# V gathered in rows of 2 KB, weights in rows of 4 KB, another plan for the transfers, and unused products in TensorE's pauses

## The chip, the cores and the metric

One core of one Trainium2 chip. The metric is the device time of one execution in microseconds (us), as a median over runs. The core has five engines that run their own instruction streams: TensorE (PE, whose weight loads the profile lists apart as PEld), VectorE (DVE), ScalarE (ACT), GpSimd (POOL) and SyncE (SP). They wait for each other by semaphores. Transfers are issued by SP, ACT or POOL and carried out by 16 DMA engines that all three share.

## What is computed

Block-sparse attention with 4 batches, 8 heads, 768 positions in 24 blocks of 32, and 64 elements per head, then an MLP from 512 to 2048 to 512:

```python
mask = np.abs(blk_i - blk_j) <= 1
mask = mask | (blk_i == 0) | (blk_j == 0) | (blk_i == n_blocks - 1) | (blk_j == n_blocks - 1)
for qb in range(n_blocks):
    for kb in sampled_blocks[qb]:            # three per block, known at run time only
        mask[qb * 32:(qb + 1) * 32, kb * 32:(kb + 1) * 32] = True
scores = np.where(mask, scale * q @ k.T, -1e9)
attn = softmax(scores)
x = (attn @ v).transpose(0, 2, 1, 3).reshape(B * S, H * D)
h = x @ w_in
out = (h / (1 + exp(-beta * h))) @ w_out
```

Each block of queries between the first and the last looks at 8 blocks of keys: the first, the last, three around it, and three drawn ones. The first and the last block of queries look at all keys.

## The kernel before

**Attention, pair by pair.** Two neighbouring blocks of queries make a pair; a batch has 11 pairs (44 in all). A pair n goes through these steps, which are also the names of the planner's tasks:

- `kg` (line 515, POOL) and `kn` (524, POOL or DVE) copy the drawn and the fixed blocks of K out of `KT` into `KG`.
- `vv` (549, SP) loads the drawn block numbers into registers, and `vg` (579, SP) gathers V's rows by DMA from a table `VT` in DRAM into `VG`: 7 transfers for most pairs, 9 for the first of a batch. `VG` is 128 partitions x 2 (the blocks of the pair) x 2 (halves of the keys) x 512, so one row of V, 1 KB, lies in one partition. The first and the last block are gathered once a batch, and `vres` (589) copies them into the other `VG` buffers.
- `sc` (595, PE) makes the scores, with a product of `ones` and `maskr` (line 600) that masks repeated blocks; `mx` (621, DVE) the maxima, `ex` (629, ACT) the exponentials, `rc` (635) and `nrm` (641, POOL or DVE) the scaling.
- `tp` (647, PE) transposes the probabilities, `ptv` (657, DVE) copies them out of PSUM, `av` (661, PE) multiplies with `VG`, and `xv` (678) writes the result to `xT`.

The first and last block of each batch go through `gs`, `gm`, `ge`, `gn`, `gt`, `gptv` and `gav` in the same manner (lines 694 to 777), with V from `Vn`.

**Getting a batch in.** Batch 0's Q, K and V are loaded as fp32 by SP at the start (line 388) and cast. Batches 1 to 3 are loaded by POOL with a cast into two staging buffers `RAW` (443), in the order V, K, Q; K shares a buffer with nothing, V and Q share the other. `perm` tasks on DVE put the rows in order (447), `trK` and `trQ` on PE transpose (460), `evK` and `evQ` copy to `KT` and `QT`. V in order (`Vn`) is written to the table `VT` by SP (`vtab`, 490 for batch 0 in two halves of the columns, 494 for the others).

**The MLP** runs over 8 groups of 256 or 512 tokens. `h` (814, PE, products at 817) makes one 128-row slice of the hidden layer out of `xT`, `tanh` (822, ACT) and `stt` (827, DVE) the activation, `y` (842, PE, products at 845) the output, `oe` (854) scales it out of PSUM, `od` (861) stores it. `w_in` and `w_out` come by POOL's DMA with a cast, in 16 pieces of 64 partitions, each row 8 KB of fp32 (417, 423). `h` waits for all eight pieces of `w_in`.

**The order** of all instructions is made on the host by a planner (`Plan`, line 36). Each task has an engine (or a choice of two), a duration, a priority and what it depends on; the planner runs a list schedule over modelled engines and 8 PSUM banks, and the kernel then issues the instructions in the planned order, engine by engine. The MLP may hold at most `moe_banks` banks (4) while attention is going on. In the planner's model all transfers pass through one ring, one after the other (`ring_at`); those of SP and ACT also take turns on 8 lanes, and POOL's large loads (`bulk`) are held back while the ring is more than `THR` us behind. The durations steer the order only; on the chip each instruction starts when its semaphores let it.

Of the kernel before, what the change touches and what calls it, by code (L numbers as in the profile page):

```python
# [22 lines left out]
class Task:  # L23
    def __init__(self, name, eng, dur, emit, deps=(), prio=0.0, lat=0.0,
                 opens=(), closes=(), moe=False, dma=0.0, slack=0.0, hw=0, bulk=None):
        self.on = {eng: dur} if isinstance(eng, str) else dict(eng)
        self.name, self.eng, self.dur, self.emit = name, None, None, emit
        self.deps = [d for d in deps if d is not None]
        self.prio, self.lat = prio, lat
        self.opens, self.closes, self.moe, self.dma = opens, closes, moe, dma  # L30
        self.slack, self.hw, self.bulk = slack, hw, bulk
        self.kind = name.rstrip("0123456789.")
        self.end = None


class Plan:
# [4 lines left out]
    def __init__(self, n_banks, moe_banks):  # L41
        self.tasks = []
        self.n_banks, self.moe_banks = n_banks, moe_banks
        self.bank = {}

# [5 lines left out]
    def run(self):  # L51
# [16 lines left out]
        ring_at = 1.0  # L68
        lanes = [0.0] * 8
# [18 lines left out]
        while done < len(tasks):  # L88
            progress = False
            for e in engines:  # L90
# [3 lines left out]
                for t in waiting[e]:  # L94
# [7 lines left out]
                    if t.bulk is not None and ring_at > now + t.bulk + 1e-9:  # L102
                        continue
# [14 lines left out]
                if t.opens:  # L118
                    bank_free.sort()
                    for name in t.opens:  # L120
                        _, i = bank_free.pop(0)
                        self.bank[name] = i
                        if t.moe:
# [6 lines left out]
                if t.hw:  # L130
                    at = now
                    for _ in range(t.hw):
                        at = max(at, lanes[issued % 8]) + t.dur / t.hw
                        ring_at = max(ring_at, at + 0.4) + t.dma / t.hw
                        end = lanes[issued % 8] = ring_at + 0.9
                        issued += 1
                    free[e] = at
                elif t.dma:
                    ring_at = max(ring_at, end + 0.6) + t.dma
                    end = ring_at + 1.1  # L140
                t.start, t.end = now, end
                order.append(t)
                heapq.heappush(events, (end, seq, t))
                seq += 1
# [8 lines left out]
            for e in engines:  # L153
                nxt += [ready_at[t] for t in waiting[e] if ready_at[t] > now + 1e-9]
                nxt += [ring_at - t.bulk for t in waiting[e]
                        if t.bulk is not None and ring_at - t.bulk > now + 1e-9]
            nxt += [f for f, _ in bank_free if f > now + 1e-9]
            if not nxt:
                raise RuntimeError("plan is stuck: " + ", ".join(
                    t.name for e in engines for t in waiting[e]))  # L160
            now = max(now, min(nxt))
            while events and events[0][0] <= now + 1e-9:
# [3 lines left out]
                done += 1  # L166
                for s in succ.get(t, ()):
# [5 lines left out]
                for b in t.closes:  # L173
                    readers[b] -= 1
                    if readers[b] == 0:
                        bank_free.append((t.end + self.HOP, self.bank[b]))
                        if b in moe_owner:
                            held_moe -= 1
        return order


@with_exitstack
def kernel(
# [52 lines left out]
    VG = [sb(f"VG{i}", [P, 2, 2, D_MODEL]) for i in range(NVG)]  # L236
# [13 lines left out]
    plan = Plan(8, 4)  # L250
# [39 lines left out]
    t_sbl = add("sbl", "ACT", 0.5, emit_sbl, prio=-200, dma=0.3, hw=1)  # L290
# [46 lines left out]
    for part, f in enumerate((emit_mask0, emit_mask1, emit_mask2)):  # L337
# [9 lines left out]
    beta_row = osb[0][0:4, :]  # L347
    ident32 = t_sb[1][0:4, 0:8].bitcast(FP32)
    FQ = N_FFC // 4
    t_beta0 = add("beta", "ACT", 0.5, lambda: nc.scalar.dma_start(  # L350
        out=beta_row, in_=moe_beta.rearrange("(q x) -> q x", q=FQ)), prio=-140, dma=0.1, hw=1)
    t_id32 = add("id32", "DVE", 0.2, lambda: nc.vector.tensor_copy(
        out=ident32, in_=identity[0:4, 0:4]), deps=[t_ident], prio=-64)

    def emit_betaT():
        for i in range(4):
            nc.tensor.transpose(out=bank("beta")[:, i * FQ:(i + 1) * FQ],
                                in_=beta_row.rearrange("q (p i) -> q i p", i=4)[:, i, :], identity=ident32)
# [3 lines left out]
        out=beta_sb[:, :].rearrange("x (q i) -> x i q", i=4),  # L362
        in0=bank("beta")[:, 0:N_FFC].rearrange("x (i q) -> x i q", i=4),
# [22 lines left out]
    for i, (nm, t, dst) in enumerate((("K", k, K16), ("Q", q, Q16), ("V", v, None))):  # L386
        for f in range(2):
            tl = add(f"ld{nm}0.{f}", "SP", 0.47, lambda i=i, t=t, f=f: nc.sync.dma_start(
                out=stage_half(i, f) if i < 2 else v_stage[:, f * HH:(f + 1) * HH, :],
                in_=src6(t, 0, f * HH, HH)), prio=-80 + i * 2 + f, dma=2.0, hw=1)  # L390
# [17 lines left out]

    w_in_r = moe_w_in.rearrange("(c p) f -> c p f", p=P)
    w_out_r = moe_w_out.rearrange("(q p i) m -> q p (i m)", p=P, i=4)  # L410
    w_in_v = w_in_sb[:, :, :].rearrange("x c (q p i) -> x c q i p", p=P, i=4)
    t_win, t_wout = [], []
    THR = 3.2
    for c in range(4):
        for f in range(2):
            ps = slice(64 * f, 64 * f + 64)
            t_win.append(add(f"win{c}.{f}", "POOL", 0.85, lambda c=c, ps=ps: nc.gpsimd.dma_start(
                out=w_in_sb[ps, c, :], in_=w_in_r[c, ps, :]),
                deps=[tch], prio=-50 + 0.2 * c + 0.1 * f, dma=1.3, bulk=THR))
    for c in range(4):  # L420
        for f in range(2):
            ps = slice(64 * f, 64 * f + 64)
            t_wout.append(add(f"wout{c}.{f}", "POOL", 0.85, lambda c=c, ps=ps: nc.gpsimd.dma_start(
                out=w_out_sb[ps, 4 * c:4 * c + 4, :].rearrange("x i m -> x (i m)"), in_=w_out_r[c, ps, :]),
                deps=[tch], prio=-49 + 0.2 * c + 0.1 * f, dma=1.3, bulk=THR))
# [7 lines left out]
    for b in range(B):  # L433
        pr = prep_prio(b)
        if b:
            vperm[b] = []
            for nm, t, raw, dst in (("V", v, RAW[0], Vn[b % 2]), ("K", k, RAW[1], K16), ("Q", q, RAW[0], Q16)):
                tr = {"K": trK, "Q": trQ}.get(nm)
                for f in range(2):
                    hs = slice(f * HH, (f + 1) * HH)  # L440
                    free = [vperm[b][f]] if nm == "Q" else [perm["QK"["VK".index(nm)], b - 1, f]] if b > 1 else []
                    tl = add(f"ld{nm}{b}.{f}", "POOL", 0.9, lambda t=t, raw=raw, b=b, f=f, hs=hs:
                             nc.gpsimd.dma_start(out=raw[:, hs, :], in_=src6(t, b, f * HH, HH)),
                             deps=free + [t_wout[-1]] if b == 1 else free,
                             prio=(-40 if b == 1 else pr - 30) + "VKQ".index(nm) + 0.5 * f, dma=2.55, bulk=THR)
# [36 lines left out]
        if b == 0:  # L482
            vperm[0], vtab[0] = [], []
            for f in range(2):
# [5 lines left out]
                vtab[0].append(add(f"vtab0.{f}", "SP", 0.45, lambda cs=cs, vt_rows=vt_rows: nc.sync.dma_start(  # L490
                    out=vt_rows[:, :, cs], in_=Vn[0][:, :, cs]),
                    deps=[vperm[0][f]], prio=-64, dma=1.3, hw=1))
        else:
            vtab[b] = [add(f"vtab{b}", "SP", 0.4, lambda b=b, vt_rows=vt_rows: nc.sync.dma_start(
                out=vt_rows, in_=Vn[b % 2]), deps=vperm[b], prio=pr + 5, dma=1.9, slack=1.0, hw=1)]
# [7 lines left out]
    for n, (b, p) in enumerate(order_pairs):  # L503
# [53 lines left out]

        def moves(vgb=vgb, vt=vt, i0=i0, first=head_v):
            if first:
                for s, blk in ((0, 0), (1, NB - 1)):  # L560
                    yield 0.25, lambda v, s=s, blk=blk: (
                        vgb[s * BLK:(s + 1) * BLK, :, 0, :],
                        bass.AP(tensor=vt.tensor, offset=vt.offset + blk * BLK * D_MODEL,
                                ap=[[D_MODEL, BLK], [0, 2], [1, D_MODEL]]))
            if i0 + 1 < NB - 2:
                yield 0.6, lambda v: (
                    vgb[BLK:P, :, 1, :],
                    bass.AP(tensor=vt.tensor, offset=vt.offset + (i0 - 1) * BLK * D_MODEL,
                            ap=[[D_MODEL, 3 * BLK], [BLK * D_MODEL, 2], [1, D_MODEL]]))
            else:  # L570
                yield 0.3, lambda v: (vgb[BLK:P, 0, 1, :], vt[(i0 - 1) * BLK:(i0 + 2) * BLK, :])
                yield 0.1, lambda v: (vgb[BLK:2 * BLK, 1, 1, :], vt[(NB - 1) * BLK:NB * BLK, :])
                yield 0.2, lambda v: (vgb[2 * BLK:P, 1, 1, :], vt[i0 * BLK:(i0 + 2) * BLK, :])
            for g in range(2):
                for r, (c, s) in enumerate(((0, 2), (0, 3), (1, 0))):
                    yield 0.1, lambda v, g=g, r=r, c=c, s=s: (
                        vgb[s * BLK:(s + 1) * BLK, g, c, :], vt[bass.ds(v[3 * g + r], BLK), :])
# [326 lines left out]
```

## Time and profile before

| | |
|---|---|
| median of 3 runs | 324.45 us (322.56 to 332.4) |
| the profiled execution | 323.59 us, span from the first to the last instruction 321.8 us |
| busy, share of the span | PE 280.7 us (87%), DVE 246.7 (77%), ACT 216.8 (67%), POOL 187.5 (58%) |
| mean granted clock of PE | 0.929 of full speed |
| chain that ended last | PE 60%, DMA 14%, DVE 12%, ACT 6% |

The profile names a group of instructions by line, engine, operation and tiles, so `PE bank L817` is the MLP's first product and `DMA VG<-VT` a gather of V. Idle time before an instruction is put down to what ended it. PE's clock is granted by a throttle, and the same product takes up to twice as long at half clock. The costliest groups on PE are the MLP's products, 97.1 us (512 products, line 817) and 90.9 us (384, line 845). DVE's are the maxima (57.5 us, line 621) and the activation (66.6 us, line 828).

### The profile page before, as it was taken

Reading aid. Unit: us, or ns where it says so; the run is one execution under the profiler, and the core shown is the slowest. Engines: PE = TensorE matmul, PEld = TensorE weight load, DVE = VectorE, ACT = ScalarE, POOL = GpSimd, SP = SyncE. Lnnn points to the kernel's source line nnn. Section 1 sums busy time; section 2 is a strip of 40 time slices with the busy share of each in tenths; the row PEclk is TensorE's granted clock in tenths of the full one; section 3 lists DMA queues with packets and bytes.
Section 4 is the critical chain, followed back from the end, with each engine's and each line's share of the span. In section 5 each row is a group of like instructions: output and inputs, shape, how many; then the busy total and the mean of one; then the engine's idle time right before and its main releaser. Section 6 shows DMA issues by size and latency. Waiting matters only on the chain.

```text
span 321.8 us, 10665 instructions
## 1 busy us (share of the span) xinstructions
PE 280.7 (87%) x3525; PEld 177.3 (55%) x3525; DVE 246.7 (77%) x572; ACT 216.8 (67%) x644; POOL 187.5 (58%) x528
## 2 busy tenths in 40 slices
PE   0845578989979699988979999999999999999994
PEld 0612366956755486556635656555665555554671
DVE  2996579878869989999987667999979975771060
ACT  1676435864968489789687669977679864772361
POOL 2479956848778456798966654756948453200000
PEclk9975557999979989999979999999999999999999
DMA  7889995998697586323777973335232333100201
GB/s 255 332 172 208 229 227 105 187 252 177 132 204 145 164 212 114 107 80 94 125 146 168 226 170 93 88 84 153 94 118 69 91 110 100 33 3 33 98 2 66
DMA packets 42211, 43.97 MB, mean 137 GB/s; under 512 B 6440, under 2 KB 37672, under 8 KB 42156
## 3 DMA queue, kind: packets, MB, share of 16 engines
q1 hardware_dynamic: 27760, 25.71, 27.1%
q0 software_dynamic: 10784, 11.27, 23.4%
q10 hardware_dynamic: 3612, 6.30, 5.4%
q8 instruction: 28, 0.46, 0.6%
q14 instruction: 27, 0.22, 0.2%
HBM read 45.10 MB, written 9.44 MB: 169 GB/s over the span
## 4 chain that ended last, share of the span: by engine, by line
PE 60%; DMA 14%; DVE 12%; ACT 6%; issue 3%; SPq 3%; POOL 1%; POOLq 0%; ACTq 0%; DVEq 0%
PE bank L845 22%; PE bank L817 21%; DMA VG<-VT 6%; PE bank L668 4%; PE bank L653 4%; DMA RAW<-in_k_dram 3%; DMA VT<-Vn 3%; SPq L582 3%; DVE ST L621 2%; ACT PP L629 2%; PE bank L463 2%; DVE g L828 2%; PE bank L610 2%; PE bank L600 2%; DMA sbl<-in_sampled_blocks_dram 1%
## 5 line engine op out<-in xcount | busy, mean ns | idle before, releaser
L641 POOL TENSOR_SCALAR PP<-PP,ST 128x256 f16<-128x256 f16 x168 | 81.3, 501 | 47.9 <-DVE ST L635 42.4
L629 ACT ACTIVATE PP<-bank,ST 128x256 f16<-128x256 f32 x176 | 81.6, 478 | 30.1 <-DVE ST L621 21.5
L817 PE MATMUL bank<-xT,w_in_sb 128*128 128x256 f16 (+1 forms) x512 | 97.1, 338 | 3.9 <-ACT PP L629 1.1
L845 PE MATMUL bank<-w_out_sb,g 128*128 128x512 f16 x384 | 90.9, 380 | 0.0
L828 DVE SCALAR_TENSOR_TENSOR g<-t,bank 128x512 f16<-128x512 f16 (+1 forms) x128 | 66.6, 546 | 22.1 <-ACT t L823 21.3
L823 ACT ACTIVATE t<-bank,beta_sb 128x512 f16<-128x512 f32 (+1 forms) x128 | 69.9, 589 | 14.3 <-PE bank L817 11.6
L817 PEld LDWEIGHTS <-w_in_sb 128*128 128x128 f16 x512 | 55.3, 116 | 30.1 <-issue 8.6
L521 POOL COPY KG<-KT 128x64 f32 x264 | 54.6, 256 | 24.6 <-PE bank L610 17.8
L621 DVE TENSOR_REDUCE ST<-bank 128x2 f32<-128x512 f32 x88 | 57.5, 678 | 7.5 <-PE bank L610 7.4
L845 PEld LDWEIGHTS <-g 128*128 128x128 f16 x384 | 34.7, 98 | 38.6 <-issue 4.1
L668 PE MATMUL bank<-PT,VG 128*128 128x64 f16 x704 | 31.8, 199 | 7.9 <-DMA VG<-VT 5.9
L668 PEld LDWEIGHTS <-VG 128*128 128x128 f16 x704 | 28.3, 102 | 16.5 <-issue 9.6
L629 ACT ACTIVATION_READ_ACCUMULATOR PP<-bank,ST 128x1 f32 x176 | 36.8, 209 | 0.0
L653 PE MATMUL bank<-identity,PP 128*128 128x128 f16 x352 | 30.9, 233 | 6.6 <-ACT xT L257 2.4
L653 PEld LDWEIGHTS <-PP 128*128 128x128 f16 x352 | 24.6, 104 | 15.9 <-issue 4.1
L657 DVE COPY PT<-bank 128x1024 f16<-128x1024 f16 x44 | 30.1, 684 | 4.1 <-PE bank L653 3.3
L259 DVE CAST xT<-bank 64x256 f16<-64x256 f32 (+1 forms) x52 | 20.6, 402 | 12.3 <-PE bank L668 7.5
L263 ACT ACTIVATE osb<-bank 128x512 f32<-128x512 f32 x24 | 14.4, 601 | 20.7 <-PE bank L845 20.7
L257 ACT CAST xT<-bank 64x256 f16<-64x256 f32 (+1 forms) x52 | 17.4, 346 | 15.4 <-DVE xT L259 6.3
L610 PE MATMUL bank<-KG,QT 64*32 64x256 f16 x704 | 20.9, 293 | 1.4 <-POOL KG L521 1.0
L726 ACT ACTIVATE PG<-bank,SG 128x384 f16<-128x384 f32 x32 | 18.4, 583 | 4.9 <-DVE SG L721 4.1
L600 PE MATMUL bank<-maskr,ones 64*32 64x192 f16 (+1 forms) x352 | 14.9, 272 | 5.7 <-ACT PP L629 5.5
(79 smaller groups left out, 256.6 us busy)
## 6 DMA issues: line engine op xcount, KB each, us to landing
VG<-VT SPq DMA_DIRECT2D x268, 32.0 KB, 2.6
VG<-VT SPq DMA_DIRECT2D x40, 192.0 KB, 2.9
out_dram<-osb ACTq DMA_DIRECT2D x20, 256.0 KB, 2.2
RAW<-in_v_dram POOLq DMA_DIRECT2D x6, 384.0 KB, 5.1
RAW<-in_k_dram POOLq DMA_DIRECT2D x6, 384.0 KB, 5.6
VT<-Vn SPq DMA_DIRECT2D x3, 768.0 KB, 6.1
RAW<-in_q_dram POOLq DMA_DIRECT2D x6, 384.0 KB, 6.5
w_in_sb<-in_moe_w_in_dram POOLq DMA_DIRECT2D x8, 256.0 KB, 5.9
```

Of the source, the lines that this page charges most:

```text
L521: nc.gpsimd.tensor_copy(out=kg32[:, g, :, (2 + r) * W:(3 + r) * W], in_=kt32[:, :, bass.ds(vals[3 * g + r], W)])
L610: nc.tensor.matmul(bk[u][hp * BLK:(hp + 1) * BLK, g * 256:(g + 1) * 256], lhsT=QT[b % 2][u * D:(u + 1) * D, hp, (i0 + g) * BLK:(i0 + g + 1 ...
L621: mx[n, u] = add(f"mx{n}.{u}", "DVE", 0.6, lambda n=n, u=u, sb_=sb_: nc.vector.tensor_reduce(out=sb_[:, 0, 2 * u:2 * u + 2], in_=bank(("S" ...
L629: nc.scalar.activation(out=pb[:, u, g, :], in_=bank(("S", n, u))[:, g * 256:(g + 1) * 256], func=AF.Exp, bias=sb_[:, 0, 2 * u + g:2 * u + ...
L641: (nc.vector if eng == "DVE" else nc.gpsimd).tensor_scalar(out=pb[:, u, g, :], in0=pb[:, u, g, :], scalar1=sb_[:, 2, 2 * u + g:2 * u + g + ...
L653: nc.tensor.transpose(out=o[:, s * P:(s + 1) * P], in_=pb[:, u, g, c * P:(c + 1) * P], identity=identity)
L657: ptv[n] = add(f"ptv{n}", "DVE", 0.61, lambda n=n: nc.vector.tensor_copy(out=PT[n % NPT], in_=bank16(("T", n))), deps=[tp[n]] + ([av[n - N ...
L668: nc.tensor.matmul(o[:, (g * NHP + hp) * 64:(g * NHP + hp + 1) * 64], lhsT=vgb[:, g, c, hp * P:(hp + 1) * P], rhs=pt[:, g, c, :, hp * BLK: ...
L817: nc.tensor.matmul(o[:, 0:TW], lhsT=w_in_v[:, c, f // 4, f % 4, :], rhs=xT[:, c, c0:c0 + TW], start=(c == 0), stop=(c == NHP - 1))
L823: lambda G=G, f=f, TW=TW, tt=tt: nc.scalar.activation(out=tt[:, 0:TW], in_=bank(("H", G, f))[:, 0:TW], func=AF.Tanh, bias=0.0, scale=beta_ ...
L828: lambda G=G, f=f, TW=TW, tt=tt, gg=gg: nc.vector.scalar_tensor_tensor(out=gg[:, f, 0:TW], in0=tt[:, 0:TW], scalar=1.0, in1=bank(("H", G, ...
L845: nc.tensor.matmul(o[:, :], lhsT=gg[:, f, s * P:(s + 1) * P], rhs=w_out_sb[:, f, :], start=(f == 0), stop=(f == N_FFC - 1))
```

## The change

Six things are changed together.

1. **V is gathered in rows of 2 KB.** Two rows of V that follow each other now lie in one partition of `VG`, so a block of 32 keys takes 16 partitions instead of 32. The number of transfers is the same, each has half as many rows of twice the length. The transposes `tp` take every second column of the probabilities to match, and `vres` copies half as many partitions of twice the length. Batch 0's table is written in one transfer once both halves are in order, instead of two.
2. **The weights come in rows of 4 KB**: 16 pieces of 128 partitions. `h` waits for the half of `w_in` that it reads. How the hidden layer is spread over slices changes with it (`NI = 2`), and with that the layout of `beta`.
3. **Batches 1 to 3 are loaded in the order K, Q, V**; V shares a staging buffer with K and waits until that is free. K and Q of batch 1 wait for the last piece of `w_out`.
4. **The planner models three rings** (SP, ACT, POOL) that share the DMA engines in proportion to their rows, and a transfer of SP or ACT isn't planned before its lane is free. `THR` compares with POOL's own backlog.
5. **`moe_banks` is 5** instead of 4.
6. **Unused products.** After planning, every pause of PE that is longer than 0.45 us and begins before 140 us of planned time gets products of `ones` with `ones` (512 columns, planned at 0.22 us each, for three quarters of the pause) into a bank that is free in the plan. Nothing reads them.

The core of the diff:

```diff
+class Rings:
+    START = {"SP": 0.4, "ACT": 0.4, "POOL": 1.0}
+    LAND = {"SP": 0.9, "ACT": 0.9, "POOL": 2.0}
+    def issue(self, ring, when, task):
+        n, each = task.dma
+        self.q[ring].append([when + self.START[ring], n * each, each, task])
+    def backlog(self, ring):
+        return sum(x[1] for x in self.q[ring])
...
-                    if t.bulk is not None and ring_at > now + t.bulk + 1e-9:
+                    if t.bulk is not None and rings.backlog("POOL") > t.bulk:
+                        continue
+                    if t.dma and e != "POOL" and lanes[issued % 8] is not None:
                         continue
...
+    def pauses(self, order, until, least):
+        at = None
+        for t in order:
+            if t.eng != "PE":
+                continue
+            if at is not None and at < until and t.start - at > least:
+                last = {}
+                for name, (a, b) in self.held.items():
+                    i = self.bank[name]
+                    if a < t.start - 1e-9:
+                        last[i] = max(last.get(i, 0.0), b)
+                i = min(range(self.n_banks), key=lambda i: last.get(i, 0.0))
+                if last.get(i, 0.0) <= at:
+                    yield t, t.start - at, i
+            at = t.start + t.dur
...
-    VG = [sb(f"VG{i}", [P, 2, 2, D_MODEL]) for i in range(NVG)]
+    VG = [sb(f"VG{i}", [P, 2, 2 * D_MODEL]) for i in range(NVG)]
...
-    plan = Plan(8, 4)
+    plan = Plan(8, 5)
...
-    THR = 3.2
...
+    THR = 2.2
+    for f in range(2):
+        fs = slice(f * D_FF // 2, (f + 1) * D_FF // 2)
+        for c in range(NHP):
+            t_win.append(add(f"win{f}.{c}", "POOL", 0.6, lambda c=c, fs=fs: nc.gpsimd.dma_start(
+                out=w_in_sb[:, c, fs], in_=w_in_r[c, :, fs]),
+                deps=[tch], prio=-50 + 0.1 * len(t_win), dma=(8, 0.174), bulk=THR))
+    for c in range(N_FFC // NI):
+        t_wout.append(add(f"wout{c}", "POOL", 0.6, lambda c=c: nc.gpsimd.dma_start(
+            out=w_out_sb[:, NI * c:NI * c + NI, :].rearrange("x i m -> x (i m)"), in_=w_out_r[:, c, :]),
+            deps=[tch], prio=-49 + 0.1 * c, dma=(8, 0.174), bulk=THR))
...
-            for nm, t, raw, dst in (("V", v, RAW[0], Vn[b % 2]), ("K", k, RAW[1], K16), ("Q", q, RAW[0], Q16)):
+            for nm, t, raw, dst in (("K", k, RAW[1], K16), ("Q", q, RAW[0], Q16), ("V", v, RAW[1], Vn[b % 2])):
...
-                    free = [vperm[b][f]] if nm == "Q" else [perm["QK"["VK".index(nm)], b - 1, f]] if b > 1 else []
+                    if nm == "V":
+                        free = [perm["K", b, f]]
+                    else:
+                        free = [vperm[b - 1][f] if nm == "K" else perm["Q", b - 1, f]] if b > 1 else [t_wout[-1]]
...
-                vtab[0].append(add(f"vtab0.{f}", "SP", 0.45, lambda cs=cs, vt_rows=vt_rows: nc.sync.dma_start(
-                    out=vt_rows[:, :, cs], in_=Vn[0][:, :, cs]),
-                    deps=[vperm[0][f]], prio=-64, dma=1.3, hw=1))
+            vtab[0].append(add("vtab0", "SP", 0.45, lambda vt_rows=vt_rows: nc.sync.dma_start(
+                out=vt_rows, in_=Vn[0]), deps=vperm[0], prio=-64, dma=(8, 0.234)))
...
-                yield 0.6, lambda v: (
-                    vgb[BLK:P, :, 1, :],
+                yield 6, lambda v: (
+                    vgb[5 * HB:P, :, :],
                     bass.AP(tensor=vt.tensor, offset=vt.offset + (i0 - 1) * BLK * D_MODEL,
-                            ap=[[D_MODEL, 3 * BLK], [BLK * D_MODEL, 2], [1, D_MODEL]]))
+                            ap=[[W2, 3 * HB], [BLK * D_MODEL, 2], [1, W2]]))
...
-                for r, (c, s) in enumerate(((0, 2), (0, 3), (1, 0))):
-                    yield 0.1, lambda v, g=g, r=r, c=c, s=s: (
-                        vgb[s * BLK:(s + 1) * BLK, g, c, :], vt[bass.ds(v[3 * g + r], BLK), :])
+                for r in range(3):
+                    yield 1, lambda v, g=g, r=r: (
+                        vgb[(2 + r) * HB:(3 + r) * HB, g, :], two(vt[bass.ds(v[3 * g + r], BLK), :]))
...
-                h64 = src[0:2 * BLK, 0:1, 0, :]
-                copy_on(eng, vgb[0:2 * BLK, :, 0, :], h64.to_broadcast([2 * BLK, 2, D_MODEL]))
+                copy_on(eng, vgb[0:BLK, :, :], src[0:BLK, 0:1, :].to_broadcast([BLK, 2, 2 * D_MODEL]))
...
+            pk = pb[:, :, :, :].rearrange("x u g (k c) -> x u g c k", c=2)
...
-                                            in_=pb[:, u, g, c * P:(c + 1) * P], identity=identity)
+                                            in_=pk[:, u, g, c, :], identity=identity)
...
-                            lhsT=vgb[:, g, c, hp * P:(hp + 1) * P],
+                            lhsT=vgb[:, g, c * D_MODEL + hp * P:c * D_MODEL + (hp + 1) * P],
...
-            th = add(f"h{G}.{f}", "PE", 4 * (TW / 2400.0 + 0.003), emit_h, deps=xdeps + t_win,
+            th = add(f"h{G}.{f}", "PE", 4 * (TW / 2400.0 + 0.003), emit_h, deps=xdeps + t_win[f // 8 * 4:f // 8 * 4 + 4],
...
+    pause = {t: (int(0.75 * gap / 0.22), i) for t, gap, i in plan.pauses(order, 140.0, 0.45)}
+    wide = bass.AP(tensor=ones.tensor, offset=ones.offset, ap=[list(ones.ap[0]), [0, 4], [1, P]])
     with tc.manual_schedule():
         for t in order:
+            n, i = pause.get(t, (0, 0))
+            for _ in range(n):
+                nc.tensor.matmul(banks[i][:, :], lhsT=ones, rhs=wide, start=True, stop=True)
             t.emit(t.eng) if len(t.on) > 1 else t.emit()
```

## The prediction

> **What bounds the kernel now.** I read the page's slices first, then TensorE's (PE's) busy time and clock by stage, then the chain of waits where PE is short of work, then the landing times of the transfers.
>
> The slices are 8 us each:
>
> ```profile
> PE   0845578989979699988979999999999999999994
> ...
> PEclk9975557999979989999979999999999999999999
> DMA  7889995998697586323777973335232333100201
> ```
>
> From slice 20 (160 us) PE is at 9 nearly to the end; before that it isn't, and in slices 3 to 5 its clock is half. The windows give the size of it:
>
> ```profile
> 16.00:20.00 4.00, 1.12 (x51) 0.61 (x36) 4.00 (x10) 1.54 (x7) 3.68 (x12) 0.98 0.69 134
> 20.00:26.80 6.80, 4.29 (x79) 1.89 (x78) 5.19 (x17) 5.32 (x23) 4.78 (x18) 0.50 0.99 195
> 26.80:42.50 15.70, 8.48 (x95) 5.04 (x96) 11.23 (x32) 7.36 (x29) 15.58 (x38) 0.50 1.06 231
> 42.50:53.70 11.20, 8.79 (x144) 6.72 (x142) 9.45 (x24) 5.96 (x23) 5.93 (x19) 0.64 0.65 151
> 53.70:57.50 3.80, 3.80 (x45) 2.48 (x41) 3.02 (x8) 2.62 (x9) 2.88 (x10) 0.55 1.11 199
> ...
> 117.50:140.00 22.50, 21.85 (x389) 14.78 (x387) 21.46 (x54) 19.88 (x66) 16.62 (x53) 1.00 0.53 116
> ...
> 170.00:316.80 146.80, 146.42 (x1617) 84.64 (x1613) 104.43 (x220) 100.40 (x282) 65.83 (x193) 1.00 0.35 95
> ```
>
> The columns after the length are PE, PEld, DVE, ACT, POOL, the clock, the DMA share, GB/s. Busy time times clock is full-rate work: stage one, 16 to 57.5 us, does 1.1 + 2.1 + 4.2 + 5.6 + 2.1 = 15.2 us of it in 41.5, and loses 26.3. The same sum for 57.5 to 170 (windows not shown) gives 96.9 of 112.5 and loses 15.6. From 170 on 0.4 is lost. So the end comes earlier by as much as is won back before 170 us; the last PE instruction ends at 316.8, and the store after it stays.
>
> What stage one waits for, from the chain:
>
> ```profile
> 16.95 0.88 DVE Vn L259
> 17.85 8.90 DMA VT<-Vn
> ...
> 30.33 6.78 DMA VG<-VT
> ...
> 37.49 7.29 DMA VG<-VT
> ...
> 51.80 1.60 DMA VG<-VT
> 53.40 0.05 issue
> 53.45 0.38 PE bank L668 x7
> 53.83 3.32 PE bank L817 x16
> ```
>
> V's table is written, then gathered, and the first h (L817) starts behind the gathers. Their landing times, from the DMA lists of 27 to 48 us and of 190 to 260 us:
>
> ```profile
> VG<-VT SPq DMA_DIRECT2D x24, 32.0 KB, 5.2
> ```
>
> ```profile
> VG<-VT SPq DMA_DIRECT2D x82, 32.0 KB, 1.9
> ```
>
> The first is beside the weights, the second with DMA lightly used: the same transfer takes 2.7 times as long.
>
> **Part by part, against the profiled run** (323.59 us, span 321.8, 0.86 under the median 324.45).
>
> *V's table for batch 0*: two writes in pieces of 512 B become one of 6 KB per partition, issued only when the second copy ends (17.83 instead of 15.7 for the first half). The like writes of later batches land in 3.3 us (80 to 112 us), 6.1 in the median, 8.9 beside loads (62 to 80 us). Counted from 17.85 they end at 21.2 and 26.8; I take 6.1, between a quiet and a crowded stretch since weights run beside it in smaller rows: 24.0 for 26.8, a gain of 2.8 (0 to 5.6).
>
> *Gathers in 2 KB rows*: their number is unchanged, 9 for the first pair of a batch, 7 for most others. From 26.8 to 48 us SP issued 31, one per 0.68 us; where it isn't held its chain shows starts at 49.32, 49.81, 50.31, one per 0.5. No more than 31 x 0.18 = 5.6 can be won, and nothing if landing stays at 5.2. [...]
>
> *The clock*: from 42.5 to 57.5 PE is busy 12.6 us and does 7.7 of work: 4.9 lost to the clock where PE is 84% busy. Before that the gathers cover it. Unused matmuls in the pauses should hold the clock: after 6.4 busy us of 7.5 (42.5 to 50) the next 2.5 us had 0.88. [...]
>
> *The cap*: 2.8 + 2.8 + 4.9 = 10.5, but DVE has 32.9 us of work in stage one's 41.5. In 117.5 to 140 it reached 0.954; at that rate this work takes 34.5. So I take 7.0, with 0 as the other end (before 42.5 a PE that is faster only waits longer). What is late next is DVE, not a transfer.
>
> *Loads of batches 1 to 3*, K, Q, V instead of V, K, Q: K of batch 1 was issued at 60.44 and 61.70 and landed at 71.6, on the chain for 9.87 us. It would now be the first load once the last weights have landed (issued at 41.2, 6.5 us to land, so 48). V becomes last; its POOL issue waits for DVE's permutation of K, with KG copies and PP scaling queued behind on POOL, as Q's issue waited for V's permutation. The table write stays on SP ahead of its gathers. Stage two holds 15.6 lost us: 12.2 with PE idle (100.3 busy of 112.5), the rest clock. DVE caps this too: 99.8 us of work at 0.954 is 104.6, so at most 7.9. The other end is a loss of 3, one gather's wait of the 1.5 us at 90 us in each of two batches. I take 5, nearer the gain because the chain shows the K load.
>
> *One more bank for the MLP* is in those bounds (PE idles 2.2 of 20 at 140 to 160). *The h wait for half of w_in*: nothing; xT ends later (h started at 53.73 right behind av; w_in's last piece was issued at 28.6 and landed within 6.8). Without that cover it would be a gain of up to 5.8, the time in which its last four pieces were issued (22.8 to 28.6), never a loss. *w in 4 KB rows*: 16 issues before and after, 0.5 us each on POOL, no change.
>
> *Copies of the shared V rows* (12): 32 partitions x 2048 for 64 x 1024. Rows give 0.41 us on DVE (x7) and 1.04 on POOL (x5); twice as many elements per lane adds 2.9 and 5.2. DVE is near full there, so I charge 1.5 (0 to 2.9).
>
> *Transposes from every second column*: PG's are strided by six and load in 125 ns against 98, yet six end in 0.50 us and eight of PP in 0.61: 56 ns apart in both. Nothing; at most 44 x 27 ns = 1.2. Two beta transposes for four: under 0.3, in the start, nothing.
>
> *Unused matmuls*: cost nothing where the pause is real. Bound: PE idles 23.9 us in 8.1 to 140 and loses 13.9 to the clock; three quarters of 37.8 is 28 us, some 130 of 0.216 us (four of L845 take 0.86). Each writes a bank, so it waits for that bank's last reader, with all of PE's queue behind it.
>
> Sum: 323.6 - 7.0 - 5 + 1.5 = 313.1. Forecast: **313 us**.
>
> **Rivals.**
>
> *More than the cap* (17%): the new order moves DVE work behind 170 us, where it idles 42 of 147. Then stage one's 10.5 and 12 of stage two count: 323.6 - 22.5 + 1.5 = 303. For: the whole order is planned anew. Against: stage two's DVE was at 0.95 and more already.
>
> *Rows don't matter* (14%): landing is a fixed part. For: 32 KB land in 1.9 us and 192 KB in 2.6 in the quiet window, so bytes and rows add little. Against: 5.2 beside the weights. Then only 2 of the clock and 3 of stage two remain: 323.6 - 5 + 1.5 = 320, inside 2%. [...]
>
> *V last holds each batch* (8%): six loads of about 2.8 us of DMA (63.1% of 18 us for four of them) from 47 on put V near 66, table and gather near 76; if the three batches then wait 4 us each, 12 gained are given back: 325. For: PE waited 1.48 us on a gather at 91.7. Against: batch 1's table landed at about 72 before, only 4 us sooner.
>
> *Slower: the unused matmuls run cold* (11%). Stage one would hold 15.2 of work and 0.75 x 26.3 = 19.7 of unused products, 34.9 at full clock. At half clock each takes twice as long; if a share h of it does, PE needs 34.9 (1 + h): over 41.5 + 7.4 = 48.9 us, which ends at the 2% line of 331, from h = 0.40 on; h = 0.6 makes 55.8 and 338. For: at 55 to 57.5 the clock was 0.52 after 3.7 busy us of 5. Against: the rise at 50 us.
>
> **How the numbers follow.** The forecast has 50% (308 to 318). A measurement of this kernel tells about 2% from no change: 318 to 331. Faster: 50 + 17 = 67%. Same: 14 + 8 = 22%. Slower: 11%. The range, 300 to 324, takes in the forecast, most of the first rival, the second and the unknown costs; the fourth (11%), half of the third (4%) and some 4% below 300 are left out.
>
> **What would show it.** Clock near 1.0 from 20 to 57 us; the table landed by 24 to 25; 32 KB gathers at 3 to 4 us in the first 50; the first h at 46 to 47; K of batch 1 landed before 60; DVE at 0.95 in stage two; matmuls of ones where PE was idle. It is wrong if the first h comes no earlier, if PE waits for V's gather at the starts of batches, or if unused matmuls stand ahead of ready work with the clock at 0.5.

## The result, and the profile after

The change made the kernel slower: 342.58 us in the median of 4 runs (340.5 to 345.75), beside 324.0 us for the kernel before on the same chip (4 runs, 322.56 to 332.4). The ratio is 1.0568, with a 95% interval of 1.0473 to 1.0663. The profiled execution took 345.75 us, its span is 344.0 us. The ratios here and below leave out runs that lie over 1.5% above the fastest of the same kernel (here 332.4 and 345.75 us, the latter being the profiled one). The kernel before differed from chip to chip (medians of 324.0 to 328.82 us), so all ratios below are to the kernel before on the same chip.

The slices of the changed kernel (8.6 us each):

```profile
PE   3928669798696899986989979993999998999995
PEclk9976967989999699998999989997899999999999
DMA  7779994975875595247667852433333223400101
```

Slices 3 to 5 (counted from 0) had a clock of 5 before and now have 6, 9 and 6. But PE, which stood at 9 from slice 21 nearly to the end, now has gaps in slices 20, 23, 27 and 33. More than half of the loss comes late, as the window from 170 us to the last work of PE shows (PE busy first, the clock third from the end):

```profile
170.00:338.30 168.30, 154.97 (x1689) 85.02 (x1687) 113.05 (x233) 104.98 (x296) 73.62 (x212) 0.97 0.36 94
```

PE was idle for 0.4 us of this stretch before, and is for 13.3 now; the span is 22.2 us longer.

The page's fourth part gives the chain that ended last, by engine and by line:

```profile
PE 43%; DMA 24%; DVE 12%; ACT 8%; SPq 6%; issue 5%; ACTq 0%; DVEq 0%
DMA VG<-VT 17%; PE bank L917 15%; PE bank L889 15%; SPq L654 6%; DMA out_dram<-osb 5%; ACT PP L700 4%; DVE ST L692 3%; PE bank L740 3%; PE bank L725 2%; DVE g L900 2%; PE bank L531 2%; ACT osb L329 1%; PE bank L952 1%; DMA g<-in_k_dram 1%; PE bank L681 1%
```

PE was 60% of this chain before and DMA 14%. Gathers of V are now 17%, and two pieces are odd there: SP's gather instruction itself (`SPq L654`) and a transfer of the output (`out_dram<-osb`). An output store should hold nobody. The waits of SP's queue, and those of PE, say whom it holds (total us, times, longest). Of the kernel before:

```profile
SPq L582 <- DMA out_dram<-osb: 8.1, 4, 4.2
```

```profile
PE bank L668 <- DMA VG<-VT: 5.9, 8, 1.5
```

Of the changed kernel:

```profile
SPq L654 <- DMA out_dram<-osb: 49.2, 14, 7.3
```

```profile
PE bank L740 <- DMA VG<-VT: 20.5, 14, 2.7
```

Of the 20.5 us that PE now waits for gathers, 17.9 lie behind 62 us, where the kernel before has 2.0 of its 5.9. Fourteen times a gather stood on SP until an output store had landed, with every later gather behind it. The chain at 81 us shows one such case whole (start, us, what):

```profile
80.98 0.50 ACT osb L329
81.48 0.02 issue
81.50 5.34 DMA out_dram<-osb
86.84 0.02 issue
86.86 3.53 DMA VG<-VT
90.39 0.05 issue
90.44 0.41 PE bank L740 x8
```

ACT scales a tile of the output, its store takes 5.34 us to land, only then is the gather issued, and `av` (L740) starts when that has landed. No data leads from the store to the gather. In the built program each of the 364 transfers of SP and ACT counts up one of eight semaphores, dealt in turn (45 or 46 to each), and each from the ninth on waits until the one that had its semaphore before has landed; POOL's 34 transfers have eight of their own. The description of the kernel before calls them the planner's 8 lanes; the built program has them too. A store waits for PE (`y`) and ACT (`oe`), so the eighth transfer behind it, mostly a gather, waits for them too, and with it every later gather on SP, though gathers are meant to run ahead of PE.

How far a gather runs ahead of a store is the order in the built program. The number of gather transfers (of 324) that stand ahead of a store (a store split in two counts twice), with two kernels of the experiments below (stores counted from 0):

| kernel | store 2 | 4 | 7 | 11 | 16 |
|---|---|---|---|---|---|
| before | 103 | 140 | 199 | 252 | 312 |
| changed | 84 | 126 | 185 | 236 | 291 |
| changed, V rows of 1 KB again | 91 | 142 | 194 | 253 | 311 |
| before, with V rows of 2 KB | 93 | 130 | 185 | 231 | 294 |

In the changed kernel each of these five stores stands 14 to 21 gather transfers earlier, two to three pairs (the others less, down to one transfer). The planner's own lists of the two kernels have little of this shift (147 gathers ahead of store 4 in both, 101 and 91 ahead of store 2): most of it arises in the built program's one order of all engines' instructions, by which the semaphores are dealt. Why the shape of the rows moves that order isn't shown.

### The profile page after: what moved, and what is told of

It reads as the page before. It is cut to its first block, busy times and chain, and to the rows that moved or that the text cites. A ratio compares the mean times of both kernels' runs of the same rounds, so it can differ in the third digit from the quotient of the medians.

```text
span 344.0 us, 10726 instructions
## 1 busy us (share of the span) xinstructions
PE 291.1 (85%) x3561; PEld 173.5 (50%) x3561; DVE 246.0 (72%) x567; ACT 216.8 (63%) x644; POOL 188.3 (55%) x533
## 4 chain that ended last, share of the span: by engine, by line
PE 43%; DMA 24%; DVE 12%; ACT 8%; SPq 6%; issue 5%; ACTq 0%; DVEq 0%
DMA VG<-VT 17%; PE bank L917 15%; PE bank L889 15%; SPq L654 6%; DMA out_dram<-osb 5%; ACT PP L700 4%; DVE ST L692 3%; PE bank L740 3%; PE bank L725 2%; DVE g L900 2%; PE bank L531 2%; ACT osb L329 1%; PE bank L952 1%; DMA g<-in_k_dram 1%; PE bank L681 1%
## 5 line engine op out<-in xcount | busy, mean ns | idle before, releaser
L712 POOL TENSOR_SCALAR PP<-PP,ST 128x256 f16<-128x256 f16 x172 | 83.3, 499 | 71.7 <-DVE ST L706 60.5
L917 PE MATMUL bank<-w_out_sb,g 128*128 128x512 f16 x384 | 94.6, 388 | 0.3 <-DVE g L900 0.3
L895 ACT ACTIVATE t<-bank,beta_sb 128x512 f16<-128x512 f32 (+1 forms) x128 | 70.7, 591 | 17.4 <-PE bank L889 10.9
L889 PEld LDWEIGHTS <-w_in_sb 128*128 128x128 f16 x512 | 49.0, 102 | 33.1 <-issue 5.5
L740 PE MATMUL bank<-PT,VG 128*128 128x64 f16 x704 | 30.6, 196 | 21.9 <-DMA VG<-VT 20.5
L740 PEld LDWEIGHTS <-VG 128*128 128x128 f16 x704 | 27.2, 100 | 32.8 <-issue 21.8
L725 PE MATMUL bank<-identity,PP 128*128 128x128 f16 x352 | 29.8, 227 | 8.8 <-DVE PTG L819 5.8
L725 PEld LDWEIGHTS <-PP 128*128 128x128 f16 x352 | 23.8, 101 | 18.7 <-POOL KG L588 6.1
L681 PE MATMUL bank<-KG,QT 64*32 64x256 f16 x704 | 19.9, 293 | 3.4 <-POOL KG L325 2.3
L809 POOL TENSOR_SCALAR PG<-PG,SG 128x768 f16<-128x768 f16 x13 | 12.0, 925 | 13.0 <-DVE SG L806 10.9
```

Source lines behind the costliest of these rows:

```text
L681: nc.tensor.matmul(bk[u][hp * BLK:(hp + 1) * BLK, g * 256:(g + 1) * 256], lhsT=QT[b % 2][u * D:(u + 1) * D, hp, (i0 + g) * BLK:(i0 + g + 1 ...
L712: (nc.vector if eng == "DVE" else nc.gpsimd).tensor_scalar(out=pb[:, u, g, :], in0=pb[:, u, g, :], scalar1=sb_[:, 2, 2 * u + g:2 * u + g + ...
L725: nc.tensor.transpose(out=o[:, s * P:(s + 1) * P], in_=pk[:, u, g, c, :], identity=identity)
L740: nc.tensor.matmul(o[:, (g * NHP + hp) * 64:(g * NHP + hp + 1) * 64], lhsT=vgb[:, g, c * D_MODEL + hp * P:c * D_MODEL + (hp + 1) * P], rhs ...
L889: nc.tensor.matmul(o[:, 0:TW], lhsT=w_in_v[:, c, f // NI, f % NI, :], rhs=xT[:, c, c0:c0 + TW], start=(c == 0), stop=(c == NHP - 1))
L895: lambda G=G, f=f, TW=TW, tt=tt: nc.scalar.activation(out=tt[:, 0:TW], in_=bank(("H", G, f))[:, 0:TW], func=AF.Tanh, bias=0.0, scale=beta_ ...
```

## The experiments

**Stores off the shared semaphores, or later among the gathers; no unused products; four banks.** Four kernels, each one edit of the changed one.

```diff
-                    nc.scalar.dma_start(out=out[base + row:base + row + P, :], in_=ob)
+                    nc.gpsimd.dma_start(out=out[base + row:base + row + P, :], in_=ob)
```

> The changed kernel with its output stores issued from POOL's queue in place of ACT's, at the same places of the same plan. Theory (gathers held by stores): in the changed kernel the gathers on SP and the stores on ACT take the same eight completion semaphores in turn, and 14 gathers stood 49.2 us on SP until a store had landed, every later gather behind them; with the stores off these semaphores SP's wait for out_dram is gone, PE's wait for VG (20.5 us) falls below 8, and the time to 320-330 us, unless POOL, which now waits for ACT's scaled rows before each store, holds its own K copies up by a few us. Rival (the rows themselves, or the 5 banks for the dense part, slow it): SP's wait goes, PE then waits for something else by as much, and the time stays at 338-345 us.

Measured: 325.53 us, ratio 1.0055 (0.9987 to 1.0123); the whole loss is gone. SP has no wait for `out_dram` ahead of a gather. PE's waits and POOL's in this kernel:

```profile
PE bank L740 <- DMA VG<-VT: 6.3, 5, 2.2
```

```profile
POOL out_dram L935 <- ACT osb L329: 45.5, 10, 15.9
```

PE's wait for V is back at the size of before. POOL now stands in front of stores in place of SP, for 11.0 us up to the last gather (issued at 267.9 us) and for 34.5 behind 278 us, where POOL has only stores left. The next kernel leaves the stores on ACT's queue and moves them back in the list of tasks, by the gathers passed:

```diff
+            if t.kind == "od":
+                held_od.append((passed, t))
+                continue
...
+            while held_od and passed >= held_od[0][0] + 18:
+                late.append(held_od.pop(0)[1])
```

> The changed kernel with each output store moved back in the order of issue by 18 gathers (two pairs), or to just before its tile is written again if that comes first; queue, semaphores and the rest of the plan unchanged. Theory (gathers held by stores): a gather then meets a semaphore whose store has had two pairs' time more to be issued, as it stood in the kernel before, so SP's wait for out_dram falls from 49 us to under 20 and the time to 322-333 us. Rival (the rows, the banks or the unused matmuls): the place of a store in the order is worth under 3 us, 338-345 us.

Measured: 328.37 us, ratio 1.0124 (0.9996 to 1.0251). The time is the theory's; of SP's wait half is left, more than the 20 us expected:

```profile
SPq L654 <- DMA out_dram<-osb: 24.1, 8, 4.8
```

With queue and semaphores unchanged, the stores' place among the gathers alone recovers most of the loss. The two other parts that could have been the loss:

```diff
-            for _ in range(n):
-                nc.tensor.matmul(banks[i][:, :], lhsT=ones, rhs=wide, start=True, stop=True)
```

> The changed kernel without its unused products; they write no output. Theory (gathers held by stores): the loss grows after 100 us and the 38 unused products lie before 147, so they are worth their own few us of PE in front of ready work (2.6 us for the first six at half clock) against what they give in clock: 338-345 us, no difference that can be told. Rival (the unused products are the loss, run cold ahead of ready work): 325-330 us.

Measured: 339.58 us (335.62, 336.98, 342.18 and 342.87; the kernel before 327.17 on that chip). By the medians 3.8% of loss is left, and so is the wait:

```profile
SPq L654 <- DMA out_dram<-osb: 41.4, 16, 6.6
```

The unused products aren't the main part of the loss. Four runs that lie this far apart can't tell whether the rest, up to 2%, goes with them.

```diff
-    plan = Plan(8, 5)
+    plan = Plan(8, 4)
```

> The changed kernel with the dense part again held to 4 of the 8 PSUM banks in the plan; the order of the whole plan moves with it. Theory (gathers held by stores): the stores stand elsewhere in the order of the gathers, so SP's wait for out_dram and the time move together, in whichever direction, at roughly 0.3-0.6 us of time for each us of wait. Rival (the fifth bank starves the attention of banks): 325-330 us with SP's wait unchanged near 49 us.

Measured: 346.81 us, ratio 1.0675 (1.0559 to 1.0791), with SP waiting 46.6 us for stores. This can't be told from the changed kernel; the fifth bank isn't the loss either. Wait and time didn't move together (2.6 us less wait, no less time), but neither moved far enough to test that.

**What the rest of the change is worth.** Both edits to the stores, on both kernels, and on the changed kernel without its unused products and with the V rows of before.

> The changed kernel with both edits: the output stores issued from POOL's queue, and each moved back by 18 gathers, so that POOL no longer stands waiting for ACT's scaled rows (45.7 us before its stores when they were moved to POOL alone, at 325.5 us). Theory (the stores were the loss, and the rest of the change saves what stage one shows): POOL's wait ahead of its stores falls under 10 us and the time to 312-321 us, under the kernel before. Rival (the rest of the change gives nothing by itself, something else is late in its place): 323-328 us, no better than with POOL waiting.

Measured: 322.2 us, ratio 0.9955 (0.9908 to 1.0002). Between the two expectations: it is a little better than with POOL waiting, not as good as the theory had it. POOL still waited 33.4 us for ACT before five stores, all behind the last gather.

> The kernel before with the same two edits to its output stores. Theory (gathers held by stores): the kernel before had 8.1 us of SP's wait for stores and 5.9 us of PE's wait for VG, so it has 2-5 us to give: 319-323 us, and the distance between this and the changed kernel with the same two edits is what the rest of the change is worth. Rival (moving the stores helps any kernel alike, the changed one had no tie of its own): 305-315 us.

Measured: 331.47 us, ratio 1.0206 (1.0078 to 1.0333). Neither expectation held, and the loss can't be put down to the edit: up to the first store (73.2 us in the profile of before) the built programs of the two kernels are the same, instruction by instruction and wait by wait, and the profiled execution is late already there. `av` of the fifth pair starts at 57.4 us, against 52.2 in the profile of before. The DMA list of 27 to 48 us (transfers, KB each, median us to landing) has this for the 32 KB gathers, which took 5.2 us there:

```profile
VG<-VT SPq DMA_DIRECT2D x15, 32.0 KB, 9.4
```

Why they landed later isn't shown by any run here. The kernel before itself ran from 320.34 to 331.39 us on that chip (29 runs). The stores' move therefore can't be priced on the kernel before.

> The changed kernel with both edits to its stores and without its 38 unused products; they write no output. If the unused products give clock in the first 60 us as they are planned to: 2-5 us slower than with them. If they stand in front of ready work at half clock (2.6 us for the first six in the changed kernel's chain): 1-4 us faster. Without the stores' tie over it, this tells them apart.

Measured: 323.54 us, ratio 1.000 (0.995 to 1.005), beside 0.9955 with the unused products. This leans to a small gain by them, less than the 2 us expected at the least, and the intervals overlap. In the window of 16 to 57.5 us the clock column is what they change, with them (first) and without:

```profile
16.00:57.50 41.50, 27.66 (x455) 18.08 (x450) 34.06 (x81) 26.39 (x97) 38.81 (x111) 0.79 0.89 191
```

```profile
16.00:57.50 41.50, 28.38 (x434) 19.22 (x433) 33.61 (x79) 25.61 (x97) 38.26 (x110) 0.63 0.90 191
```

The clock rises from 0.63 to 0.79, and the first `h` comes at 48.4 us in place of 49.2.

> The changed kernel with both edits to its stores, and V gathered in rows of 1 KB into the arrangement of the kernel before (with its half as large copies of the shared rows and its transposes of whole halves), in the same plan. If rows of 2 KB shorten nothing, the 32 KB gathers land in the same median as with 2 KB rows within 0.3 us, and the time is 0-3 us lower by the smaller copies (0.1-0.2 us each, 16 of them on DVE or POOL). If the rows are worth what the prediction gave them (a table and gathers landing sooner, some 3 us of stage one), it is 2-5 us slower.

Measured: 322.18 us, ratio 0.9996 (0.9939 to 1.0053), beside 322.2 and 0.9955. The same plan with 2 KB rows (first) and with 1 KB rows, DMA lists of 27 to 48 us:

```profile
VG<-VT SPq DMA_DIRECT2D x25, 32.0 KB, 4.8
```

```profile
VG<-VT SPq DMA_DIRECT2D x23, 32.0 KB, 5.0
```

Here a gather of 32 KB takes about as long in 2 KB rows as in 1 KB rows, 4.8 against 5.0 us.

**One part alone, both ways round.** If the place of the stores is the cause, then undoing the part that moved them must bring the time back with the stores on ACT, and doing that part alone must bring the loss to the kernel before. The edit, here as made to the kernel before (the others of the V rows go with it, as in the diff of the change):

```diff
-                    yield 0.1, lambda v, g=g, r=r, c=c, s=s: (
-                        vgb[s * BLK:(s + 1) * BLK, g, c, :], vt[bass.ds(v[3 * g + r], BLK), :])
+                    yield 0.1, lambda v, g=g, r=r: (
+                        vgb[(2 + r) * HB:(3 + r) * HB, g, :], two(vt[bass.ds(v[3 * g + r], BLK), :]))
```

> The changed kernel with only the V rows undone (gathers of 1 KB rows into the arrangement of before, with its copies and transposes), the output stores on ACT as in the change, the same plan. In the built program of this kernel the stores stand some two pairs later among the gathers than in the changed kernel, as they do in the kernel before, though the plan is the same. Theory (the gathers' place against the stores decides, and the 2 KB rows shifted it): SP's wait for out_dram falls from 49 us to under 20 and the time to 320-328 us, where the same undoing gave nothing (322.2 against 322.2 us) with the stores on POOL's queue. Rival (the plan's new order or the loads are what holds the gathers): 337-345 us.

Measured: 320.23 us, ratio 0.9769 (0.9714 to 0.9823). With only its V rows undone the change is a gain of 2.3% on this chip, where the kernel before was slower than on the others (its fastest run 325.1 us, against 320.34 to 322.56). SP's wait and PE's:

```profile
SPq L654 <- DMA out_dram<-osb: 11.4, 6, 2.9
```

```profile
PE bank L741 <- DMA VG<-VT: 6.9, 8, 2.0
```

> The kernel before with only the V rows of the change (gathers of 2 KB rows, the larger copies, the strided transposes), its own plan, loads, weights and banks. In its built program the stores stand one to two pairs earlier among the gathers than in the kernel before. Theory (the 2 KB rows by themselves bring the loss, through the stores' place): SP's wait for out_dram rises from 8.1 us to 25-50 and the time to 332-348 us. Rival (the loss needs the new plan or the order of the loads): 322-328 us.

Measured: 346.68 us, ratio 1.0569 (1.0506 to 1.0631): the V rows alone cost the kernel before as much as the whole change did.

```profile
SPq L587 <- DMA out_dram<-osb: 42.0, 12, 6.4
```

```profile
PE bank L673 <- DMA VG<-VT: 17.6, 13, 5.9
```

Not all of it is the tie. The first `h` came at 61.9 us against 53.7 before, ahead of any store; of the span's 25.6 us more, 8.2 were there by then, and the other 17.4 came afterwards. Of the 17.6 us that PE waited for gathers, 12.2 are in the early part. This part is of the kind seen with the stores moved on the kernel before (first `h` at 59.5), where the program up to there was unchanged, and stays open like that.

In the later part, where SP stands on stores, PE waits 5.4 us for gathers and longer for POOL:

```profile
PE bank L750 <- POOL PG L742: 10.1, 2, 8.9
```

The longest of these waits, 8.9 us, is the tie by another way. The chain leads from a store through the gathers to POOL's copies of the shared rows (`VG L259`), and from there to PE:

```profile
229.63 0.61 ACT osb L263
230.26 1.99 DMA out_dram<-osb
...
235.44 2.55 DMA VG<-VT
...
238.15 0.81 POOL VG L259
...
242.93 0.89 POOL PG L742
...
243.86 0.84 PE bank L750 x6
```

**The version that keeps everything.**

```diff
-            def emit_od(ob=ob, base=base, row=row):
+            def emit_od(ob=ob, base=base, row=row, q=nc.gpsimd if nout < 15 else nc.scalar):
```

> The changed kernel with the stores on POOL's queue and moved back while gathers are still to come, and on ACT's queue again from the 16th store on, when the last gather is issued. In the run with all stores on POOL, POOL waited 33.4 us for ACT before 5 of them, nearly all behind the last gather, and the end came 3.3 us later behind the last dense products than in the kernel before. Theory: those 3 us come back, 317-320 us, 1.5-3% under the kernel before. Rival (the end of a store costs the same from either queue): 321-323 us.

Measured: 319.53 us, ratio 0.9766 (0.9707 to 0.9824), as the theory had it: behind the last dense product the end takes 4.9 us, where it took 7.9 with all stores on POOL. This and the changed kernel with V rows of 1 KB and its stores on ACT (320.23 us) can't be told apart; both are faster than the two kernels that were compared. The ratio is to the slower kernel before of that chip; beside the first chip's 324.0 us, 319.53 would be 1.4% less. What went wrong can be mended from either end: the rows or the stores.

```diff
-            for nm, t, raw, dst in (("K", k, RAW[1], K16), ("Q", q, RAW[0], Q16), ("V", v, RAW[1], Vn[b % 2])):
+            for nm, t, raw, dst in (("V", v, RAW[0], Vn[b % 2]), ("K", k, RAW[1], K16), ("Q", q, RAW[0], Q16)):
```

> The same kernel with the loads of the later batches in the order of before (V, K, Q), and the buffers that go with it; the plan is made anew. The prediction gave stage two 5 us; with the tie of the stores gone the run had 9 us at pair 7 (64.7 against 73.8), 1.3 at pair 11 and 4.6 at pair 15: it was given back where batch 1 begins, where SP waited 6.9 us for DVE ahead of the table and 5.1 for the table. If V last is what gives it back: pair 11 two to five us earlier and the time 2-5 us lower. If V first delays K and with it the scores: no gain, 0-4 us higher.

Measured: 333.91 us, ratio 1.0188 (1.0125 to 1.025), 14 us above the kernel with V last. Both expectations missed: V first costs much more than either said. Batch 1 did get its table sooner (80.0 us; with V last its final piece of V landed at 85.3 and the table was written after that), yet its first `av` came at 104.9 us, not at 99.9. No one wait accounts for the 14 us. With the plan made anew for each, the order K, Q, V is shown to be the better one here, not why.

## Why the prediction was wrong

The forecast was 313 us, with 11% for slower; it came out at 342.58, outside the range. **The step that failed is the one on gathers in 2 KB rows**: it counted their number, their issue and their landing, and left out what stands ahead of a gather on the semaphore it shares. The front text had taken the eight lanes for a matter of the planner, and the working never asked which transfers they tie together in the built program. The sum had no term for it, and none of the rivals was this one. The term measured: 342.58 us with the tie and 320.23 with only the rows undone, a difference of 22 us; by the ratios on their two chips, 5.7% over and 2.3% under the kernel before, it is about 8%, some 26 us of 324. That the shape of the rows costs nothing by itself is shown with the stores on POOL (322.2 and 322.18 us). The profile of before had the line that shows it, 8.1 us of SP's wait for `out_dram`; the working made no use of SP's waits beyond stage one.

The other steps, read where the tie is off:

- *V's table*: right and too small. The write took 4.15 us, where I took 6.1, and ended at 21.97 (24.0 forecast, 26.8 before): 4.8 us.
- *Gathers' landing*: wrong in the size of its term, 2.8 us in the sum, for which no run shows a ground. What the runs showed in its place: the 32 KB gathers took 4.9 us in the changed kernel's list of 27 to 48 us, 5.2 before, in spite of 1,382 packets on SP's queue where there were 2,020. The rival "rows don't matter" was right on this. Of the 4.8 us at the table only 1.1 was left at the first `av` (33.4 against 34.5): the chain below is landing after landing.

```profile
17.80 4.15 DMA VT<-Vn
21.97 0.34 SPq L654
22.31 0.05 issue
22.36 6.37 DMA VG<-VT
28.75 6.39 DMA VG<-VT
...
37.14 5.25 DMA VG<-VT
...
46.63 5.57 DMA VG<-VT
```

- *The clock*: 0.75 in stage one (0.79 with the stores off the tie, 0.59 in the kernel before), not 1.0. What the clock does to one product: 16 of `h` took 3.32 us at 53.83 us of the profile of before, 0.21 each at a clock of 0.53, and 8 at 95.11 us took 0.87, 0.11 each at 1.00. There were 38 unused products, not some 130: the planner sees few of the pauses that the chip has, and the bound from the chip's pauses was no estimate of it. The rival in which they run cold isn't what happened: without them the changed kernel is still at 339.58, and with the stores off the tie they lean to a gain. Six do stand in front of the K transposes, at 7.34 us of the chain for 2.56 us, 0.43 each, where five at 13.13 us take 1.08, 0.22 each; the clock column has 1.00 for both, so what slows the six isn't shown.
- *Stage one in all*: forecast 7.0 us. The first `h` came 4.5 us earlier (49.2 against 53.7), and 3.3 to 5.4 earlier in the runs with the tie loosened or off. The direction was right.
- *Stage two*: forecast 5, not found. In the best version the first `h` of the fourth group starts at 140.3 us against 142.6, less than stage one alone had gained. K of batch 1 landed at 67.8, not before 60: it waited for the last of `w_out` (landed at 55.5) as the diff says, and I had put that at 48. V last isn't shown to be the cause, as the plan with V first is worse. DVE, which was to be the cap at 0.95, was busy 100.9 of the 112.5 us in the best version, 0.90.
- *Copies of the shared rows*: charged 1.5. All 12 went to DVE, 8.5 us of its time where it had 3.1. With 1 KB rows and half of these copies the time was no lower, so what they cost can't be measured.

Two slips of the working change nothing in it: PE is at 9 from slice 21, not 20, and its busy time from 57.5 to 170 us adds up to 100.9, not 100.3, so 11.6 us were idle, not 12.2.

Without the tie the change gives 0.5% (0 to 0.9, all stores on POOL) to 2.3% (1.8 to 2.9, the best version, on the chip with the slower kernel before), where the forecast, 313 against 323.6, was 3.3%. Both versions lie in the forecast's range and on its side. The missing term is the largest error and not the only one: of the 10.5 us of gain that were forecast, some 1.5 to 7.5 are found.

## What to carry to other kernels

A queue can wait for more than its data (here SP stood 49.2 us for output stores that no gather needs). Where transfers share completion semaphores, list for each transfer on a critical queue which one had its semaphore before; if that one belongs to work downstream (an output store), the prefetch is tied to the consumer, and any edit that shifts their order, even one of the shape of rows, can turn slack into a stall (8.1 us of SP's wait for stores in the kernel before, 42.0 with nothing but its V rows changed). Read the waits of the issuing queues, not of the compute engines alone: a transfer that should hold nobody is the mark. Here eight semaphores are shared by all transfers of SP and ACT, and taking the stores off them was worth 17 us (342.58 to 325.53, ratios 1.0568 and 1.0055).

## What the runs showed that was not expected

- The same program can take its first 50 us at two speeds: 32 KB gathers beside the weights took 5.2 us in the profile of before and 9.4 in the kernel before with its stores moved, which is the same up to its first store, with the first `h` at 53.7 and 59.5 us. The cause is open.
- A store of 256 KB from POOL's queue landed in 2.8 us (median of six at 190 to 260 us, stores on POOL, V rows of 1 KB), one from ACT's in 2.0 (six in the same stretch of the changed kernel). With all stores on POOL at their own places, POOL stood 45.5 us in front of ten of them; with the stores moved back, putting only the last ones back to ACT shortened the end behind the last dense product from 7.9 to 4.9 us.
- Rows of twice the length changed nothing in landing: 2.0 us against 1.9 in the quiet stretch of 190 to 260 us, 4.9 against 5.2 beside the weights.
